# Retention and WaveMLP on one core: the first third of the instruction order written anew

## The chip, the cores and the metric

The kernel runs on one core of a Trainium2 chip. Its time is the device time of one execution in microseconds (us), as the median of several runs. The core has five engines with instruction streams of their own: PE (TensorE, the matrix unit), DVE (VectorE), ACT (ScalarE), POOL (GpSimd) and SP (SyncE, which only starts transfers here). Transfers run on 16 DMA engines and are started by SP and ACT (hardware queues) or POOL (a software queue, which here also turns float32 into bfloat16 on the way). Engines wait for each other through semaphores.

## The reference

Two layers follow each other. The first is a recurrent retention over q, k and v of shape (4 batches, 8 heads, 768 positions, 64 numbers); the second is a WaveMLP over its output, 4 x 768 x 512.

```python
for t in range(S):                                   # retention, per head, gamma = 1 - 2^(-5-h)
    state = gamma * state + outer(k[t], v[t])
    y[t] = scale * q[t] @ state
theta = x @ w_theta                                  # x: the heads side by side, 512 wide
u = x + w_tok_r @ (x * cos(theta)) + w_tok_i @ (x * sin(theta))
out = u + relu(u @ w_ch)
```

## The kernel before, in words

**Units of the retention.** The work of the retention is cut into 24 units, numbered from 0. Unit n belongs to batch n // 6, to a stretch of 256 positions ((n // 2) % 3) and to four of the eight heads (n % 2). A unit loads three tiles of 256 KB: keys (`Lk`), queries (`Lq`) and values (`Lv`), all through `load_unit` (L154 to L161). Keys and queries share a pool of 16 buffers (`kqf`), values have 9 (`vf`). The tiles are turned into bfloat16 and, where it is needed, scaled by the decay: `ck`, `cq`, `cqs` (tile `kqb`) and `cv` (tile `vb`). PE transposes keys and queries (`Tk`, `Tq`, L316), a copy `E` brings them to `kqT`, `A` (L346) makes the products of keys and queries, `m` (L355, DVE) masks them, `ST` (L373) makes the unit's contribution to the state, `S0` and `S1` add it up, `SB` writes the state as a bfloat16 matrix `sbd`, `I` (L411) applies it to the queries, and `Y` (L423) adds the part inside the unit. `XB` (a plain copy) or `XA` (a product with the decay table `qx`, L441) writes the result as half a block of `xT`.

**Blocks of the WaveMLP.** The two units 2p and 2p + 1 give two blocks of 128 positions, C = 2p and 2p + 1, over all 512 columns. For a block, `Tx` and `Ex` (or the transposing transfer `Dx`) turn `xT` round into `x_sb`; `Hh` (L469) multiplies by theta's weight; `CN` (L476, ACT) takes sine and cosine; `z` (L483) multiplies by x. The token weights are two matrices of 768 x 768. Their rows come in six transfers `Pw(r, g)` (L180 to L185, tile `row`) with r = 0 for the real, 1 for the imaginary matrix, and g = 0, 1, 2 for row blocks 0, 1 to 2 and 3 to 5. `Tw(r, t0)` (L491, tile `w_ps`) transposes one row block, `Ew` copies it. `M(t, s)` (L509, tile `y_ps`) is one of the six steps that make output block t of a batch; `u`, `Tu`, `Du`, `O` (L536), `f` and `SO` finish a block and store it. `Pth` (L173) loads theta's weight, `Pch` the channel weight. `Z` (L278) is a pair of matmuls on zeros that nothing reads.

**Constants.** `const9` and `const8` (both through L233, ACT) fill the decay table `qx` for positions 256 to 767 and 0 to 255. `const7` (L252, ACT) is a first sine, ahead of which ACT loads the table for sine.

**What sets the order.** There is no scheduler. The table `ORDER` (L22 to L86) is a list of such calls; a letter at the end of a name says which engine does it (a ACT, v DVE, p POOL, s SP). Each engine runs its instructions in the order in which the table names them, and waits with each until its inputs are there and its buffer is free. So a call that waits holds up whatever stands behind it on the same engine, its transfers too.

**Queues and buffers around the change.** The loads that SP and ACT start take eight semaphores in turn, so a load is started only when the one eight before it has landed. The weight transfers go through POOL's own queue, in the order of POOL's instructions. `th_ps`, `y_ps` and `o_ps` share two banks, so the bank of a theta product comes free when both `CN` of its block are done. The state of a unit must be in `sbd` before its `I`, and the two `SB` before it may stand on different engines.

Of the kernel before, what the change touches and what calls it, by code (L numbers as in the profile page):

```python
# [31 lines left out]
CN.0.0 Tq.5 Hh.1 Tk.5 SB.4.0.p SB.4.1.a Pw.0.1 Hh.2 m.4 E.5.v I.4 Y.4 ST.5 ck.6.a Tk.6 Tx.2 cq.6.a
CN.1.1 CN.1.0 XA.4.1 A.5 XA.4.0 m.5 Lq.9.s Ex.2.v S0.5.v z.0.p Tq.6 E.6.a CN.2.0 cv.6.p Hh.3
SB.5.0.v Tx.3 Tw.1.0 z.1.v SB.5.1.a Ew.1.0.v Ex.3.a CN.2.1 A.6 I.5 Y.5 ST.6 XA.5.0 z.2.v Tw.0.0
CN.3.0 Tx.4 CN.3.1 Ew.0.0.v S0.6.v XA.5.1 Ex.4.v Hh.4 CN.4.0 CN.4.1 Tw.0.1 M.0.1 Pw.1.1 z.3.v M.0.0
Tw.0.2 Pw.1.2 Ew.0.2.a SB.6.1.a Hh.5 z.4.p SB.6.0.p Lk.9.a M.0.3 ck.7.p cqs.7.p M.0.2 CN.5.1 CN.5.0
cq.8.a m.6 Ew.0.1.v Tw.1.1 Tw.1.2 Ew.1.1.v Lv.9.s M.0.4 M.1.0 Tx.5 Ew.1.2.v M.1.1 S1.6 Tk.7 M.1.4
Pch Ex.5.v z.5.v cv.7.v Tq.8 Tq.7 M.1.2 E.7.a M.0.5 I.6 Y.6 ST.7 A.7 ck.8.a u.0 S0.7.v m.7 XA.6.1
SB.7.1.a M.1.5 M.1.3 XA.6.0 Tw.1.3 M.2.5 Pw.0.2 M.2.3 u.1 S1.7 Tk.8 M.2.1 M.2.0 SB.7.0.v Ew.1.3.a
Tu.0 I.7 cv.8.p E.8.a cv.9.p Y.7 ST.8 A.8 cqs.9.v ck.9.v M.2.4 Du.1 Lk.10.s Eu.0.a XB.7.1.a XB.7.0.v  # L40
S0.8.v SB.8.0.v M.2.2 Tx.6 Tq.9 Tk.9 Lv.10.a cv.10.p ck.10.p Lq.10.s S1.8 u.2 m.8 O.0 E.9.a SB.8.1.a
Hh.6 Tw.1.4 I.8 Y.8 A.9 CN.6.0 Du.2 Lq.14.s CN.6.1 Ex.6.v f.0 ST.9 Tw.0.3 Hh.7 Ew.1.4.v Ew.0.3.a
S0.9.v Tw.0.4 M.3.0 Tw.1.5 CN.7.0 CN.7.1 M.3.2 Dx.7 M.3.1 M.3.5 M.3.3 Lv.12.s Lk.12.s Ew.1.5.v
XA.8.1 Ew.0.4.v Lq.12.s M.3.4 u.3 S1.9 Tw.0.5 Tk.10 M.4.5 cqs.10.p XA.8.0 m.9 M.4.3 Tq.10 SB.9.1.a
SB.9.0.a I.9 O.2 Lq.11.s Lk.11.s E.10.a Lk.15.s Ew.0.5.v Lk.14.s Y.9 ST.10 A.10 z.7.p Lv.11.s
XB.9.1.a XB.9.0.a f.2 M.4.0 O.1 M.4.1 cqs.14.p m.10 S0.10.v f.1 cq.11.a ck.12.v M.4.4 M.4.2 Tu.3
Eu.3.a Dx.9 SB.10.0.a cqs.12.p u.4 Hh.9 Tq.11 ck.11.v Tu.4 z.6.v Eu.4.v ck.15.v M.5.0 M.5.4 Tk.11
E.11.a SB.10.1.p cv.11.p M.5.2 M.5.3 I.10 M.5.5 M.5.1 Lq.13.a A.11 Y.10 ck.14.v ST.11 CN.9.1 CN.9.0
SO.0.a Hh.8 u.5 S0.11.v z.9.v XB.10.0.v m.11 Dk.12 Tx.8 Tq.14 O.4 Lv.13.a SB.11.0.a Lq.15.s Lk.13.s
CN.8.1 Lk.18.a XB.10.1.a CN.8.0 SB.11.1.p cv.12.p Lq.16.s I.11 Tk.14 Ex.8.v A.12 Y.11 ST.12 f.4  # L50
Lv.15.s O.3 z.8.p E.14.a XA.11.0 XA.11.1 Hh.10 S0.12.a f.3 SB.12.0.v Tx.10 Tu.5 CN.10.1 Dx.11
Ex.10.v cq.13.p Lk.16.s Lv.17.s Hh.11 SO.2.s CN.10.0 m.12 S1.12 z.10.v Tk.15 M.6.1 M.6.2 M.6.0 M.6.3
CN.11.0 CN.11.1 M.7.3 Lk.17.a ck.13.a M.7.4 M.7.0 M.6.4 Dk.13 M.7.1 z.11.v SB.12.1.a M.6.5 SO.3.s
A.14 M.7.2 Eu.5.v I.12 Lv.14.s u.6 cqs.15.v M.7.5 M.9.3 Tq.15 ck.17.a E.15.a m.14 SO.4.a Lq.17.s
Lq.18.s Lk.21.s ck.16.a M.9.0 M.9.5 M.9.1 M.9.4 Lq.19.a M.9.2 Du.6 cv.13.v u.7 M.8.0 u.9 Y.12
cv.14.p ST.13 A.13 O.5 cq.16.p XB.12.1.a XB.12.0.a M.8.1 S0.13.a S1.13 M.8.4 M.8.3 SB.13.0.a
SB.13.1.p m.13 I.13 ck.18.a Y.13 ST.14 A.15 f.5 cq.17.v Lv.18.a M.8.5 M.8.2 XA.13.0 XA.13.1 S0.14.v
SB.14.0.p Lv.16.s Hh.13 S1.14 u.8 Tx.12 M.10.1 cv.15.p cv.17.p SB.14.1.p M.10.0 M.10.4 cqs.18.v
M.10.5 CN.13.0 CN.13.1 Hh.12 CN.12.1 I.14 m.15 Y.14 CN.12.0 ST.15 S0.15.v XB.14.1.a SB.15.0.a M.10.3
cv.16.v Dk.16 Dk.17 Du.7 Dx.13 M.10.2 Dk.18 O.6 SB.15.1.p XB.14.0.v S1.15 I.15 Y.15 ST.16 SO.5.a  # L60
cv.18.p f.6 S0.16.v A.16 M.11.4 SB.16.1.p M.11.1 Lq.21.a Ex.12.a z.12.p SB.16.0.a Lk.19.s Lk.20.s
XB.15.0.a u.10 z.13.p XB.15.1.a m.16 O.7 Du.10 I.16 Y.16 ST.17 f.7 A.17 Tu.8 Hh.15 CN.15.1 CN.15.0
Dx.14 M.11.2 Tx.15 Lv.22.s SO.7.s M.11.0 M.11.5 S0.17.v SB.17.0.p M.11.3 XA.16.1 m.17 XA.16.0
# [24 lines left out]

# [545 lines left out]
```

## Time and profile before

| what | value |
|---|---|
| time, median of 3 runs | 165.86 us (165.68 to 165.93) |
| span of the profiled execution | 164.0 us, granted TensorE clock 0.999 |
| busy in the span: PE, DVE, ACT, POOL | 153.7, 113.1, 79.6, 76.9 us |
| read from HBM, written | 25.69 MB, 6.29 MB |
| channel of POOL's weight transfers (q0) | 3.41 MB, 12.1% of 16 DMA engines' span |
| hardware loads and stores (q1), transposing transfers (q10) | 23.73 MB, 7.47 MB |

The profile follows one execution. Its span runs from the first to the last instruction; the device time of that same execution isn't on the page, so the median stands beside the span, 1.9 us above it. A row of the timeline gives start, duration, engine, line of the code, operation, the tile written and the tiles read, and in brackets how long the engine had been idle and for whom. In a row of windows each engine has its busy time and, in brackets, its instructions; then come the granted TensorE clock, the share of the DMA engines (above 1 where transfers of several queues overlap) and GB/s. A row of the chain of waits is start, length and what the end of the program hung on in that stretch. Busy times of PE overlap from one matmul to the next, so the chain's lengths are the better measure of what a group of matmuls adds.

### The profile page before, as it was taken

The page shows a single profiled execution, that of the slowest core. Times are in us where ns is not written, and L with a number is a line of the kernel's source. Part 1 is how long each engine was busy: PE and PEld are TensorE (multiplying, and loading weights), DVE is VectorE, ACT ScalarE, POOL GpSimd, SP SyncE. Part 2 cuts the span into 40 slices and gives each one's busy share as a digit, 9 for nine tenths or more (in the row PEclk, how much of TensorE's full clock was granted, in tenths as well). Part 3 has the DMA queues.
Part 4 walks back from the last instruction along what each step waited for, and adds up shares of the span by engine and source line. Part 5 has one row for each costly group of instructions (what it writes and reads, how often), then busy time and mean ns, then how long its engine had stood idle before and what let it go on. Part 6 is the DMA issues. An engine that isn't in the chain of part 4 may idle for free.

```text
span 164.0 us, 4889 instructions
## 1 busy us (share of the span) xinstructions
PE 153.7 (94%) x2001; PEld 87.0 (53%) x2030; DVE 113.1 (69%) x210; ACT 79.6 (49%) x142; POOL 76.9 (47%) x109
## 2 busy tenths in 40 slices
PE   5997789999999999999999999999999999999992
PEld 1455556656666655654454565555555545455550
DVE  3298677977993896994879895789867760244462
ACT  4976889983658245762433725832341616000020
POOL 7957279186306733730307599951469104500000
PEclk9999999999999999999999999999999999999999
DMA  4999999999999999949999896999999438514455
GB/s 118 297 290 251 272 284 250 279 217 280 210 214 257 290 170 222 310 115 285 318 259 199 173 247 182 187 169 301 213 271 131 96 83 211 160 68 123 104 209 203
DMA packets 69062, 34.93 MB, mean 213 GB/s; under 512 B 26416, under 2 KB 66096, under 8 KB 69040
## 3 DMA queue, kind: packets, MB, share of 16 engines
q1 hardware_dynamic: 56032, 23.73, 67.4%
q10 hardware_dynamic: 10320, 7.47, 16.1%
q0 software_dynamic: 2688, 3.41, 12.1%
q8 instruction: 16, 0.26, 0.7%
q14 instruction: 6, 0.05, 0.1%
HBM read 25.69 MB, written 6.29 MB: 195 GB/s over the span
## 4 chain that ended last, share of the span: by engine, by line
PE 73%; DMA 12%; ACT 5%; POOL 4%; issue 2%; DVE 1%; DVEq 0%; SPq 0%; POOLq 0%; ACTq 0%
PE y_ps L509 35%; PE o_ps L536 12%; PE th_ps L469 9%; DMA row<-in_moe_w_tok_i_dram 5%; DMA kqf<-in_k_dram 4%; DMA kqf<-in_q_dram 4%; PE r_ps L423 3%; ACT qx L233 3%; PE at_ps L346 2%; PE r_ps L411 2%; PE kq_ps L316 2%; PE w_ps L491 2%; PE y_ps L561 2%; PE r_ps L373 1%; PE u_ps L521 1%
## 5 line engine op out<-in xcount | busy, mean ns | idle before, releaser
L509 PE MATMUL y_ps<-z,wti 128*128 128x512 bf16 x131 | 49.6, 379 | 1.0 <-issue 1.0
L509 PE MATMUL y_ps<-z,wtr 128*128 128x512 bf16 x131 | 49.7, 379 | 0.3
L483 POOL TENSOR_TENSOR z<-cs,x_sb 128x1024 bf16<-128x1024 bf16 x12 | 25.4, 2124 | 17.6 <-DMA x_sb<-xT 10.0
L355 DVE TENSOR_TENSOR at<-at_ps,mask 128x1024 bf16<-128x1024 f32 x24 | 29.2, 1216 | 0.6 <-PE at_ps L346 0.5
L308 POOL TENSOR_TENSOR vb<-vf,vsc 128x512 bf16<-128x512 f32 x17 | 18.0, 1063 | 21.3 <-DMA vf<-in_v_dram 21.0
L542 DVE SCALAR_TENSOR_TENSOR ot<-o_ps,u 128x512 f32<-128x512 f32 x23 | 15.8, 688 | 12.9 <-PE o_ps L536 12.8
L469 PE MATMUL th_ps<-wth,xT 128*128 128x512 bf16 x88 | 23.9, 379 | 0.5
L516 DVE TENSOR_TENSOR u<-y_ps,x_sb 128x512 bf16<-128x512 f32 x23 | 15.8, 688 | 12.0 <-PE y_ps L509 11.9
L536 PE MATMUL o_ps<-wch,uT 128*128 128x512 bf16 x88 | 23.2, 379 | 0.4 <-issue 0.2
L476 ACT ACTIVATE cs<-th_ps,zerob 128x512 bf16<-128x512 f32 x24 | 16.4, 684 | 12.7 <-PE th_ps L469 8.2
L476 ACT ACTIVATE cs<-th_ps,halfpi 128x512 bf16<-128x512 f32 x24 | 16.3, 684 | 10.5 <-issue 4.3
L139 POOL CAST sbd<-s 64x256 bf16<-64x256 f32 (+1 forms) x21 | 10.0, 476 | 22.9 <-DVE s L391 20.5
L509 PEld LDWEIGHTS <-wtr 128*128 128x128 bf16 x138 | 13.5, 98 | 12.7
L509 PEld LDWEIGHTS <-wti 128*128 128x128 bf16 x138 | 13.5, 98 | 11.9 <-DVE wti L139 0.2
L137 ACT COPY kqT<-kq_ps 128x1024 bf16<-128x1024 bf16 x12 | 12.1, 1012 | 10.9 <-PE kq_ps L316 10.9
L137 ACT CAST kqb<-kqf 128x512 bf16<-128x512 f32 x17 | 10.2, 619 | 8.0 <-DMA kqf<-in_k_dram 7.2
L469 PEld LDWEIGHTS <-xT 128*128 128x128 bf16 x96 | 8.9, 98 | 8.3
L536 PEld LDWEIGHTS <-uT 128*128 128x128 bf16 x92 | 8.4, 98 | 8.6
L316 PE MATMUL kq_ps<-ident,kqb 128*128 128x128 bf16 x120 | 11.2, 219 | 0.4 <-ACT kqb L137 0.2
L278 PE MATMUL zz<-zero 128*128 128x512 bf16 x27 | 9.5, 481 | 2.0 <-DVE zero L192 1.9
L423 PE MATMUL r_ps<-at,vb 64*64 64x128 bf16 x384 | 10.0, 221 | 1.1 <-DVE at L355 1.1
L316 PEld LDWEIGHTS <-kqb 128*128 128x128 bf16 x120 | 8.2, 98 | 4.5 <-POOL kqb L139 0.6
(77 smaller groups left out, 204.6 us busy)
## 6 DMA issues: line engine op xcount, KB each, us to landing
vf<-in_v_dram SPq DMA_DIRECT2D x20, 256.0 KB, 6.0
kqf<-in_k_dram SPq DMA_DIRECT2D x19, 256.0 KB, 5.3
kqf<-in_q_dram SPq DMA_DIRECT2D x17, 256.0 KB, 5.1
out_dram<-ot ACTq DMA_DIRECT2D x12, 256.0 KB, 3.0
out_dram<-ot SPq DMA_DIRECT2D x11, 256.0 KB, 3.1
kqf<-in_q_dram ACTq DMA_DIRECT2D x7, 256.0 KB, 5.4
kqf<-in_k_dram ACTq DMA_DIRECT2D x5, 256.0 KB, 5.0
vf<-in_v_dram ACTq DMA_DIRECT2D x4, 256.0 KB, 6.1
```

Of the source, the lines that this page charges most:

```text
L137: nc.scalar.copy(dst, src)
L308: engines[e].tensor_mul(in_blocks(vb), by_token(raw["vf", n]), _bcast_last(K["vsc"][:, i, :, h * HU:(h + 1) * HU], D))
L316: nc.tensor.transpose(st["kq_ps", n][:, 4 * w + x, :], st["kqb", n][:, w, x * P:(x + 1) * P], K["ident"])
L355: nc.vector.tensor_mul(at.rearrange("p g j a t -> p (g j) (a t)"), st["at_ps", n].rearrange("p g j a t -> p (g j) (a t)"), _bcast_mid(K["m ...
L423: nc.tensor.matmul(st["R", n + 1][c][g * D:(g + 1) * D, j * P:(j + 1) * P], st["vb", n][rows, lo:lo + D], st["at", n][rows, g, j, a, :], s ...
L469: nc.tensor.matmul(th_ps, st["xT", C][:, j, :], K["wth"][:, j, :], start=(j == 0), stop=(j == 3))
L476: nc.scalar.activation(st["cs", C][:, w, :], st["th_ps", C], AF.Sin, bias=K["zerob" if w else "halfpi"], scale=1.0)
L483: engines[e].tensor_mul(st["z", b][:, c], st["cs", C], _bcast_mid(x_of(C), 2))
L509: nc.tensor.matmul(st["y", t], K["wT"][r][:, s0, t0 * P:(t0 + 1) * P], st["z", b][:, s0, r, :], start=(done == 0 and r == 0), stop=(done = ...
L516: nc.vector.tensor_add(st["u", t], st["y", t], st["x", b][:, t0, :])
L536: nc.tensor.matmul(o_ps, st["uT", t][:, j, :], K["wch"][:, j, :], start=(j == 0), stop=(j == nD - 1))
L542: nc.vector.scalar_tensor_tensor(st["ot", t], st["o", t], 0.0, st["u", t], ALU.max, ALU.add)
```

## The change

The calls of the first third of `ORDER`, up to the run `A.12 Y.11 ST.12 f.4` (about 69 us in the trace of before), stand in another order. Both tables hold the same matmuls and the same number of calls; behind that point only three copies have another engine (unit 11's `XA` became `XB`, unit 12's second `XB` moved from ACT to DVE). Some calls in the first third change the engine or the form too: the plain cast of the queries (`cq`) and the scaled one (`cqs`), together with `XB` and `XA`, swap for units 1, 4, 8 and 11, and the `z` of blocks 0 and 4 moves from POOL to DVE while that of blocks 3 and 6 moves from DVE to POOL. The table has five lines fewer, so each line number below it is lower by five.

```diff
-Tk.1 E.1.a Y.0 ST.1 XB.0.1.a cqs.2.v Z.34 S0.1.v S1.1 cv.2.p SB.1.0.a Pth Lq.3.s Z.18 XB.0.0.v Tq.2
-CN.1.1 CN.1.0 XA.4.1 A.5 XA.4.0 m.5 Lq.9.s Ex.2.v S0.5.v z.0.p Tq.6 E.6.a CN.2.0 cv.6.p Hh.3
+Y.0 A.1 m.1 Lk.4.s Pth Lq.4.s cqs.3.p Lv.4.s ST.1 Lq.5.s Tk.2 XB.0.0.a cqs.2.p ck.3.p XB.0.1.a Tq.2 Z.18
+Tk.5 SB.4.0.a m.4 Tx.2 Hh.2 Lv.6.s Pw.1.1 Ex.2.v XB.3.1.a ck.6.p SB.4.1.a CN.0.1 I.4 z.1.v E.5.a Tx.3 Y.4
```

The order of the loads changes with it. Before, SP and ACT start them as Lv.0 Lk.0 Lq.0 Lv.1 Lq.1 Lk.1 Lq.4 Lk.4 Lq.2 Lk.2 Lv.2 Lq.3 Lk.3 Lv.3 Lv.4 and then unit by unit up to unit 8, whose values are called for just ahead of `E.4`. Now it is Lv.0 Lk.0 Lq.0 Lv.1 Lq.1 Lk.1 Lv.2 Lq.2 Lk.2 Lq.3 Lv.3 Lk.3 Lk.4 Lq.4 Lv.4 and on, and the loads of units 7 and 8 are called for behind the transfer `Pw.1.1`; unit 8's keys come last, on ACT, behind three loads of units 9 and 10.

On POOL, around theta's weight, the order before was this (`vb` is a unit's values in bfloat16, `kqb` its keys and queries; the number of a tile counts the tiles made, so it differs between the two kernels):

```order
L308 TENSOR_TENSOR vb_253<-vf_143,vsc_131 128x512
L308 TENSOR_TENSOR vb_317<-vf_255,vsc_131 128x512
L173 DMA wth_99<-in_moe_w_theta_dram 128x4x512
L139 CAST kqb_406<-kqf_384 128x512
L302 TENSOR_TENSOR kqb_406<-kqf_321,qsc_130 128x512
```

And now:

```order
L303 TENSOR_TENSOR vb_182<-vf_143,vsc_131 128x512
L303 TENSOR_TENSOR vb_193<-vf_177,vsc_131 128x512
L168 DMA wth_99<-in_moe_w_theta_dram 128x4x512
L297 TENSOR_TENSOR kqb_316<-kqf_226,qsc_130 128x512
L297 TENSOR_TENSOR kqb_252<-kqf_184,qsc_130 128x512
L134 CAST kqb_316<-kqf_274 128x512
L134 CAST kqb_434<-kqf_311 128x512
```

The scaled cast of unit 2's queries (kqb_252) has come to POOL, behind unit 3's; a cast of the state and the scaling of unit 1's queries, which stood on POOL ahead of the first row shown before, have left it.

On POOL again, from the first transfer of token rows on, the order before was this (row10 and row11 are the imaginary rows of block 0 and of blocks 1 and 2, row00 and row01 the real ones, row13 the imaginary rows of blocks 3 to 5):

```order
L182 DMA row10_106<-in_moe_w_tok_i_dram 128x768
L182 DMA row00_103<-in_moe_w_tok_r_dram 128x768
L139 CAST sbd00_95<-s2_427 64x4x64
L182 DMA row01_104<-in_moe_w_tok_r_dram 128x2x768
L483 TENSOR_TENSOR z_754<-cs_627,x_sb_498 128x1024
L308 TENSOR_TENSOR vb_764<-vf_467,vsc_131 128x512
L182 DMA row11_107<-in_moe_w_tok_i_dram 128x2x768
L182 DMA row13_108<-in_moe_w_tok_i_dram 128x3x768
```

And now:

```order
L177 DMA row10_106<-in_moe_w_tok_i_dram 128x768
L134 CAST kqb_563<-kqf_336 128x512
L177 DMA row00_103<-in_moe_w_tok_r_dram 128x768
L303 TENSOR_TENSOR vb_640<-vf_520,vsc_131 128x512
L177 DMA row01_104<-in_moe_w_tok_r_dram 128x2x768
L177 DMA row11_107<-in_moe_w_tok_i_dram 128x2x768
L134 CAST kqb_665<-kqf_607 128x512
L134 CAST sbd10_97<-s2_553 64x4x64
L177 DMA row13_108<-in_moe_w_tok_i_dram 128x3x768
```

Between row01 and row11 stood block 0's `z` and unit 6's values; now nothing stands there, and two casts of unit 5 have come ahead of row01.

On ACT, around the first sine, the order before was this (`kqT` is a unit's transposed keys and queries, `one` the tile of the first sine):

```order
L233 ACTIVATE qx_134<-pos_148,lscale_83,lgp_150 128x256 x4
L137 CAST kqb_193<-kqf_172 128x512
L157 DMA kqf_197<-in_q_dram 128x4x128
L157 DMA kqf_217<-in_k_dram 128x4x128
L137 COPY kqT_272<-kq_ps_240 128x1024
L137 CAST xT_306<-r_ps_260 128x256
L137 CAST sbd10_97<-s2_313 64x2x64 x2
L137 CAST kqb_308<-kqf_250 128x512
L252 ACT_TABLE_LOAD
L252 ACTIVATE one_356<-zerob_87,halfpi_85 128x1
L137 CAST xT_326<-r_ps_358 128x256
```

And now:

```order
L132 COPY kqT_358<-kq_ps_338 128x1024
L228 ACTIVATE qx_134<-pos_148,lscale_83,lgp_150 128x256 x4
L132 CAST sbd01_96<-s2_250 64x4x64
L132 COPY kqT_465<-kq_ps_381 128x1024
L132 COPY x_sb_500<-x_ps_454 128x512
L247 ACT_TABLE_LOAD
L247 ACTIVATE one_518<-zerob_87,halfpi_85 128x1
L152 DMA kqf_523<-in_q_dram 128x4x128
L132 CAST sbd11_98<-s2_362 64x4x64
```

The second part of the decay table has moved behind unit 2's copy `E` (kqT_358), and the table load with the first sine behind unit 3's (kqT_465) and block 0's `Ex`.

More of the change, by code (lines that the diff above doesn't have):

```diff
@@ L34 @@
[L34 to L63, printed above, removed]
@@ new lines @@
+SB.19.1.p SB.19.0.v M.13.0 z.17.v cqs.21.v XB.18.0.v S1.19 z.16.v cv.20.v M.12.3 M.12.2 M.13.5 Lv.21.s
+M.13.1 m.19 M.12.4 M.12.5 I.19 M.13.4 Y.19 ST.20 u.12 A.20 Dk.21 XA.19.1 S0.20.v XA.19.0 ck.22.a cq.22.a
+SB.20.1.p cv.22.p M.14.3 M.14.5 M.14.1 M.14.4 M.14.2 M.14.0 SB.20.0.p u.13 m.20 S1.20 Hh.19 I.20 Y.20
+SO.10.s Lq.23.s Lk.23.s cv.21.v u.14 A.21 ST.21 CN.19.0 CN.19.1 S0.21.v M.15.3 M.15.5 S1.21 m.21 XA.20.1
+Hh.18 CN.18.1 CN.18.0 Dx.18 Dk.22 ck.23.a M.15.4 M.15.2 SB.21.0.p M.15.1 M.15.0 SB.21.1.v Lv.23.s Du.12
@@ L86 @@
+Tuh.1 Euh.1 f.21 O.20 f.20 Oh.0 Oh.1 SO.21.a SO.22.s SO.20.s fh.0 SOh.0 fh.1 SOh.1 Z.31
 """.split()
```

81 lines of the change are left out of this document (50 added, 31 removed).

## The prediction

> **What bounds the kernel now.** I read the page's first lines, then busy time by stretches, then the chain of waits, then PE's timeline.
>
> ```profile
> span 164.0 us, 4889 instructions
> PE 153.7 (94%) x2001; PEld 87.0 (53%) x2030; DVE 113.1 (69%) x210; ACT 79.6 (49%) x142; POOL 76.9 (47%) x109
> ```
>
> PE is the bound over the whole. The windows (length; PE, PE's loads, DVE, ACT, POOL; granted clock, DMA share, GB/s) say where it is not full:
>
> ```profile
> 7.40:21.80 14.40, 11.77 (x280) 8.24 (x283) 10.46 (x20) 10.67 (x20) 8.81 (x13) 1.00 1.20 274
> 21.80:28.70 6.90, 6.62 (x112) 4.00 (x108) 5.66 (x11) 6.22 (x11) 5.99 (x8) 1.00 1.18 262
> 28.70:36.30 7.60, 7.36 (x110) 4.64 (x109) 6.21 (x15) 6.93 (x13) 3.18 (x4) 1.00 1.15 250
> 36.30:69.20 32.90, 32.13 (x511) 20.30 (x515) 26.47 (x52) 18.34 (x31) 15.67 (x17) 1.00 1.14 243
> 69.20:159.00 89.80, 88.48 (x987) 47.01 (x996) 60.32 (x105) 32.13 (x62) 37.19 (x38) 1.00 0.86 186
> ```
>
> PE idles 2.6 us up to 21.8 (matmuls on zeros are in its busy time too), then 0.3, 0.2 and 0.8 us. From 36 us on it is nearly full, so whatever the new order is to win must be won ahead of about 36 us. The DMA engines are saturated there (share 1.14 to 1.20). The chain of waits (start, length, what) leaves PE between 9.3 and 35.7 us:
>
> ```profile
> 9.27 6.62 DMA kqf<-in_k_dram
> ...
> 16.32 5.75 DMA kqf<-in_q_dram
> ...
> 22.15 1.14 ACT kqb L137 x2
> 23.28 1.17 ACT cs L476 x2
> 24.53 1.17 POOL z L483
> ...
> 26.61 0.98 POOL vb L308
> 27.60 8.04 DMA row<-in_moe_w_tok_i_dram
> ```
>
> Loads release casts on ACT, these the sine and cosine, these block 0's z on POOL, and behind that product and unit 6's values POOL starts the second imaginary rows at 27.60. They take 8.04 us. PE's timeline shows who waits for them, and four other marks:
>
> ```profile
> 20.16 0.38 PE L411 MATMUL r_ps<-kqT,sbd 128*128 128x128 bf16 x4 [0.44 <-ACT xT L137]
> ...
> 21.79 1.04 PE L469 MATMUL th_ps<-wth,xT 128*128 128x512 bf16 x3
> ...
> 32.41 0.38 PE L509 MATMUL y_ps<-z,wtr 128*128 128x512 bf16 x1
> ...
> 35.68 0.84 PE L491 MATMUL w_ps<-ident,row 128*128 128x128 bf16 x12 [0.18 <-DMA row<-in_moe_w_tok_i_dram]
> ...
> 42.82 0.39 PE L316 MATMUL kq_ps<-ident,kqb 128*128 128x128 bf16 x4
> ```
>
> These are I.3, the first theta product, the first token product, Tw.1.1 (which waits for the rows of 27.60) and unit 8's keys.
>
> **The measure.** The work of PE is the same in both kernels, so I compare its lag: the start of a mark less PE's own work ahead of it. If the lag at 36 us falls by x and the dense part stays dense, the end moves by x. What a group adds to PE is its length in the chain:
>
> ```profile
> 36.53 0.86 PE y_ps L509 x4
> 37.39 0.22 PE x_ps L455 x4
> ...
> 40.12 0.35 PE r_ps L423 x16
> 40.47 0.12 PE r_ps L373 x16
> 40.59 0.23 PE at_ps L346 x16
> ...
> 41.79 0.34 PE w_ps L491 x6
> ...
> 47.61 0.86 PE th_ps L469 x4
> ```
>
> So T, Tx and I cost 0.22, Y 0.35, ST 0.12, A 0.23, Tw 0.34, Hh 0.86, and M (two matmuls) 0.43. I leave out the zeros, which fill gaps. Before, 14 Tk and Tq (3.08), 7 ST (0.84), 7 A (1.61), 6 Y (2.10), six I of which two are half (1.10), 5 Tx (1.10), 5 Hh (4.30) and 3 Tw (1.02) stand ahead of the first token product: 15.15 us, a lag of 32.41 - 15.15 = 17.26. Up to Tw.1.1 come 4 M, a Tw and an Hh, 2.92: the lag is 35.68 - 18.07 = 17.61. Now one Tw fewer stands ahead of the first token product (14.81), and 3 M, 2 Tw, an Hh and a Tx (3.05) stand between, 17.86 in all.
>
> **The change, part by part.**
>
> *Loads and theta's weight.* All bytes still come, at the same rate. Unit 2 and unit 3 come in order where unit 4 had come ahead of unit 2, and theta's weight is issued about 2.5 us sooner. By the rows below it would land near 17 us instead of 12.54 + 6.8 = 19.3; its first reader, Hh.1, I put near 20.4. Before, Hh.0 at 21.79 did not wait for it either, so I cost this at nothing; what hides it is the retention of units 2 and 3. The price is that unit 3's keys land some 3 us later, about 16.4 by my count of 0.9 us a load (256 KB at 274 GB/s), near the time when E.3 wants them.
>
> ```profile
> 12.54 0.93 POOL L173 DMA_DIRECT2D wth<-in_moe_w_theta_dram  x1
> ```
> ```profile
> wth<-in_moe_w_theta_dram POOLq DMA_DIRECT2D x1, 512.0 KB, 6.8
> ```
>
> *ACT.* The second part of the decay table and the table load now lie between E.2 and I.3:
>
> ```profile
> L476 ACT ACTIVATE cs<-th_ps,zerob 128x512 bf16<-128x512 f32 x6 | 4.1, 683 | 0.0
> L137 ACT COPY kqT<-kq_ps 128x1024 bf16<-128x1024 bf16 x4 | 4.0, 1011 | 1.4 <-PE kq_ps L316 1.4
> ...
> L233 ACT ACTIVATE qx<-pos,lscale,lgp 128x256 f32<-128x256 f32 x4 | 2.1, 584 | 0.0
> ...
> L137 ACT COPY x_sb<-x_ps 128x512 bf16<-128x512 bf16 x3 | 1.8, 585 | 0.0
> L137 ACT CAST sbd<-s 64x256 bf16<-64x256 f32 x4 | 1.6, 402 | 2.1 <-DVE s L391 2.1
> ...
> L137 ACT CAST xT<-r_ps 128x256 bf16<-128x256 f32 x4 | 1.5, 370 | 0.1
> ```
> ```profile
> 13.05 1.28 ACT L252 ACT_TABLE_LOAD   x1
> 14.35 0.29 ACT L252 ACTIVATE one<-zerob,halfpi 128x1 f32<-128x1 f32 x1
> ...
> 33.81 0.80 ACT L137 COPY wtr<-w_ps 128x768 bf16<-128x768 bf16 x1 [0.36 <-PE w_ps L491]
> ```
>
> I put unit 2's transposed queries at 13.6, so E.2 ends near 15.0 and the decay table near 17.0. SB.2.0 and the keys of unit 3 let E.3 start near 17.7. From there ACT has E.3 1.01, Ex.0 0.59, the table load 1.28 and the first sine 0.29, SB.3.0 0.40, two XB 0.74 and SB.3.1 0.40: 4.71 us, ending at 22.4, or 22.2 since neighbours overlap a little. I.3 then starts at 22.2 against 20.16, 2 us later. But Hh.1 now stands ahead of it, and PE's work from I.3 to the first token product is smaller: I 0.66, Y 1.05, ST 0.36, A 0.69, four Hh 3.44, four T 0.88, three Tx 0.66, two Tw 0.68 = 8.42, which alone gives 30.6. ACT decides instead: a token product needs a bank that CN.3.0 frees, and behind SB.3.1 ACT has eight CN (5.46), three XB (1.11), three SB (1.20), two E (2.02) and a weight copy (0.80): 10.6 us. One after the other that ends at 32.8; with starts about 0.1 us sooner than the ends before them, at 31.0. ACT was busy 6.93 of 7.60 us in 28.7 to 36.3, so waits are few; I take 31.7, with 31.0 and 32.8 as ends. The lag there is 31.7 - 14.81 = 16.89 against 17.26, a gain of 0.37.
>
> *Rows.* Without z.0 and unit 6's values ahead of it, Pw.1.1 is issued at about 25.0 instead of 27.60. Its price is 8.04, so it would land near 33.0, up to 36.1 if it shares the engines with more loads (an estimate: 3 us more). Tw.1.1 wants it at 31.7 + 3.05 = 34.75. Were it there, the lag would be 16.89 and the gain 17.61 - 16.89 = 0.72. The two preceding real rows are wanted 0.86 us behind the first token product and may be late too, so I leave 0.22 us for these waits: gain 0.50.
>
> *z and casts between POOL and DVE.* z.0 left the chain, where it cost 1.17 us. Its reader, the first token product, comes at 31.7, and DVE (5.66 of 6.90 us busy in 21.8 to 28.7) has it done by then: nothing. A z on DVE behind late sines could hold a mask and with it a Y; that belongs to the ends above.
>
> *Units 7 and 8.* Behind unit 8's keys stand ck.8 and Tk.8. Up to these keys 30 loads (7.86 MB), theta's weight (0.52) and five row transfers (1.77) must come: 10.16 MB. At 274 GB/s and less in the windows above (3.95, 1.81 and 1.90 MB from 7.4 to 36.3) and about 1.5 MB ahead of 7.4 (an estimate, three quarters of the rate behind it), 9.1 MB are there at 36.3, and the rest at 243 GB/s at 40.6. With a cast on POOL of 0.6 us (an estimate between the copies above) Tk.8 could start at 41.3. Before it started at 42.82, with the gain it is wanted near 42.4. So I cost it at nothing, with about 1 us to spare.
>
> **Sum.** -0.37 at the first token product, -0.35 that the rows no longer add, +0.22 for row waits: -0.50. The executions' span is 164.0 and the median 165.86, 1.9 around it, which both kernels have: 163.5 and 165.4.
>
> **A rule against it.** The five row transfers and the loads meet on the same DMA engines. From 31.4 to 36 us (packets, MB, share of the engines), and one load issued there (KB, us to landing):
>
> ```profile
> q0 software_dynamic: 501, 0.75, 88.9%
> q1 hardware_dynamic: 542, 0.27, 26.3%
> ...
> kqf<-in_k_dram ACTq DMA_DIRECT2D x1, 256.0 KB, 6.9
> ```
>
> While rows are under way, the loads get 0.27 MB in 4.6 us, a fifth of the 1.3 MB that they would get alone at 274 GB/s. The Trainium skill ("DMA: Bandwidth & Descriptors", "Queues, rings and completion order") says that each DMA engine takes turns between its queues packet by packet. The trace agrees: 501 and 542 packets, though the row packets carry three times the bytes. By that rule the loads of units 7 and 8, now called for behind the rows, cannot push ahead, and unit 8's keys come late; that is the first rival.
>
> **The rivals.**
> - *R1, slower: unit 8's keys are late.* If Pw.1.2 and the next rows (Pw.0.2) run back to back from 33 to about 40 us (1.18 MB at 0.75 MB in 4.6 us is 7.2 us), the loads get 0.42 MB in that time. Unit 8's keys and the three loads ahead of them are 1.05 MB, so 0.6 MB are left, 2.3 us at 274 GB/s: landing near 42.5 and Tk.8 at 43.3, in the worst case 44.5. For it speaks that the load issued in that stretch took 6.9 us; against it that eight loads are under way by then. It decides from a landing at about 41.8 on. A wait of 0.7 to 2 us, less the gain: 166.1 to 167.4, at its middle 166.7. Chance 0.20.
> - *R2, slower: ACT bounds the stretch up to 32 us.* If E.3 waits for unit 3's keys to 19 us, I.3 starts at 23.5 and the first token product at 33 instead of 31.7; beyond 32.1 nothing is gained there. With 0.6 to 1.3 us more than I took: 166.0 to 166.7, at its middle 166.3. For it speaks that the decay table, the table load and the first sine (3.7 us) stand between E.2 and I.3 on ACT; against it that Hh.1 fills PE. Chance 0.16.
> - *R3, no change: the rows come as late as before.* If the second imaginary rows land at 35.5 all the same, because the ones ahead take the queue, the lag is as before: 165.9. For it speaks the 0.75 MB in 4.6 us. Chance 0.12.
> - *R4, more gain:* no wait for rows and ACT at its lower end, 31.0: 17.61 - (31.0 - 14.81) = 1.4 us at most, 164.4. Chance 0.06.
>
> **How the numbers follow.** A measurement tells about 0.2% (0.33 us) from no change. My forecast, 165.4, has 0.40 for itself, about 165.0 to 165.7; with R4 faster holds 0.44 after taking off 0.02 for its edge at 165.53. R3 and these edges are the 0.14 of no change. R1, R2 and 0.06 for a stall that I don't see (the stretch from 43 to 69 us is written anew too, where PE idles 0.8 us; or a granted clock below the 1.00 of all windows) make slower 0.42. The range goes from R4's end, 164.4, to R1's, 167.4; the likeliest alone has 165.0 to 165.7.
>
> **What would show it.** In the profile of the changed kernel: the table load between 19 and 21 us; I.3 near 22.2 and the first token product near 31.7, ahead of 32.41; the second imaginary rows issued near 25.0 and no idle time ahead of Tw.1.1, at about 35.0; Tk.8 near 42.4 with no idle time, and PE's idle time from 36 to 69 us at 0.8 us or less. I am wrong if I.3 comes behind 23, if a wait for kqf or kqb of unit 7 or 8 stands on PE between 37 and 44 us, or if the windows behind 43 us show new idle time on PE.

## The result and the profile after

The changed kernel takes 167.08 us (166.90 to 167.13, 4 runs) beside 165.77 us for the kernel before in the same runs: a ratio of 1.0081 (95% interval 1.0067 to 1.0096), 1.3 us slower. The prediction said 165.4 and faster. The profiled execution has a span of 165.4 us against 164.0; it is the one of the four with a low granted clock (0.99 on average; the others have 0.997 to 1.00, and take 166.90 to 167.13 us like it).

The first lines of the page after, with the granted clock in 40 slices:

```profile
span 165.4 us, 4921 instructions
PE 156.2 (94%) x2030; PEld 87.1 (53%) x2030; DVE 114.1 (69%) x206; ACT 81.0 (49%) x145; POOL 79.1 (48%) x110
...
PEclk9996999999999999999999999999999999999999
```

Busy shares are as before; PE has 2.5 us more, partly because the trace of before holds 29 matmul records fewer. New is the 6 in the fourth slice of the clock. The windows after, in the columns of the prediction:

```profile
7.40:21.80 14.40, 12.00 (x247) 7.58 (x247) 9.68 (x18) 9.72 (x17) 9.42 (x12) 0.88 1.21 278
21.80:28.70 6.90, 5.71 (x140) 3.81 (x138) 5.94 (x13) 6.63 (x15) 5.39 (x10) 1.00 1.19 280
28.70:36.30 7.60, 7.30 (x109) 4.66 (x107) 6.05 (x13) 6.35 (x10) 3.54 (x4) 1.00 1.16 224
36.30:43.00 6.70, 6.68 (x92) 3.99 (x91) 4.76 (x9) 2.55 (x4) 2.01 (x4) 1.00 1.16 273
43.00:69.20 26.20, 26.10 (x375) 15.91 (x373) 21.86 (x40) 17.14 (x30) 14.69 (x13) 1.00 0.96 217
```

PE idles 1.2 us from 21.8 to 28.7 us where it had idled 0.3, and ahead of 21.8 its matmuls run at a clock of 0.88 on average. From 36 us on it is full. So the loss too lies ahead of 36 us. PE's timeline has the waits; these are the ones over 0.5 us, and then the first token product and Tw.1.1 (the last row):

```profile
9.55 0.42 PE L341 MATMUL at_ps<-kqT 64*64 64x128 bf16 x16 [0.67 <-ACT kqT L132]
11.63 0.62 PE L311 MATMUL kq_ps<-ident,kqb 128*128 128x128 bf16 x8 [1.12 <-ACT kqb L132]
...
23.14 0.40 PE L406 MATMUL r_ps<-kqT,sbd 128*128 128x128 bf16 x4 [0.63 <-ACT sbd L132]
28.44 0.51 PE L486 MATMUL w_ps<-ident,row 128*128 128x128 bf16 x6 [0.56 <-DMA row<-in_moe_w_tok_i_dram]
...
33.44 0.38 PE L504 MATMUL y_ps<-z,wtr 128*128 128x512 bf16 x1
...
36.49 0.50 PE L486 MATMUL w_ps<-ident,row 128*128 128x128 bf16 x6
```

With the prediction's own counts the lag at the first token product is 33.44 - 14.81 = 18.63 against 17.26, 1.37 us more, and the span is 1.4 longer. At Tw.1.1 it is 36.49 - 17.86 = 18.63 against 17.61: no wait for the second imaginary rows any more, but 1.0 us more lag; the other 0.4 us come behind it, with no single wait that stands out. The chain of waits names what came before each (its longer pieces):

```profile
4.79 5.62 DMA kqf<-in_k_dram
...
10.44 1.15 ACT kqb L132 x2
...
18.54 0.41 POOL sbd L134
...
19.02 1.04 POOL vb L303
20.07 0.97 POOL kqb L297
21.03 0.98 POOL vb L303
22.01 6.39 DMA row<-in_moe_w_tok_i_dram
...
28.44 0.52 PE w_ps L486 x6
...
31.55 1.85 ACT cs L471 x3
...
33.44 1.02 PE y_ps L504 x4
```

Two transfers stand in it that the sum didn't have. The first is unit 1's keys. Before, SP started them at 2.40 us and they landed at 8.76; now ACT starts them behind the first part of the decay table, at 4.79, behind the values of unit 2 and the queries of unit 3 on the DMA engines, and they land at 10.41. PE waits 1.12 us for their cast (the line of 11.63 above). The second is the first imaginary rows (row10). POOL waits 2.89 us with unit 2's state cast for the state, and three products stand between that cast and the transfer, which lands at 28.40 instead of 26.45.

```profile
18.54 0.40 POOL L134 CAST sbd<-s 64x256 bf16<-64x256 f32 x1 [2.89 <-DVE s L386]
```

Two corrections to the text ahead of the prediction. In the table of the profile before, the queue q10 is ACT's queue (28 loads and stores there before, 32 after, with 7.47 and 8.52 MB), not the transposing transfers. And the order of the loads that the text on the change gives is that of the calls in the table, not that of the starts. In the trace of before, ACT starts unit 4's queries and keys only at 8.79 and 9.27, behind the decay table and behind the starts of unit 2's and unit 3's queries and keys (5.18 to 8.30). In the trace after, unit 1's keys stand ahead of unit 2's values and unit 3's queries in the table, but those are started at 2.41 and 4.56 and the keys at 4.79.

### The profile page after: what moved, and what is told of

Read it like the earlier page. It is cut to its first block, busy times and chain, and to the rows that moved or that the text cites. A ratio compares the mean times of both kernels' runs of the same rounds, so it can differ in the third digit from the quotient of the medians.

```text
span 165.4 us, 4921 instructions
## 1 busy us (share of the span) xinstructions
PE 156.2 (94%) x2030; PEld 87.1 (53%) x2030; DVE 114.1 (69%) x206; ACT 81.0 (49%) x145; POOL 79.1 (48%) x110
## 3 DMA queue, kind: packets, MB, share of 16 engines
q10 hardware_dynamic: 12816, 8.52, 18.1%
q0 software_dynamic: 2688, 3.41, 11.7%
## 4 chain that ended last, share of the span: by engine, by line
PE 78%; DMA 7%; ACT 4%; POOL 4%; DVE 3%; issue 1%; DVEq 0%; ACTq 0%; POOLq 0%
PE y_ps L504 36%; PE o_ps L531 12%; PE th_ps L464 9%; DMA row<-in_moe_w_tok_i_dram 4%; PE r_ps L418 4%; PE kq_ps L311 3%; DMA kqf<-in_k_dram 3%; PE at_ps L341 3%; PE w_ps L486 2%; PE r_ps L406 2%; PE y_ps L556 2%; PE r_ps L368 2%; POOL vb L303 1%; ACT cs L471 1%; ACT kqT L132 1%; PE x_ps L450 1%
## 5 line engine op out<-in xcount | busy, mean ns | idle before, releaser
L504 PE MATMUL y_ps<-z,wtr 128*128 128x512 bf16 x138 | 52.4, 380 | 0.2
L504 PE MATMUL y_ps<-z,wti 128*128 128x512 bf16 x138 | 52.4, 379 | 0.0
L464 PE MATMUL th_ps<-wth,xT 128*128 128x512 bf16 x96 | 24.5, 379 | 0.0
L471 ACT ACTIVATE cs<-th_ps,zerob 128x512 bf16<-128x512 f32 x24 | 16.4, 686 | 12.8 <-PE th_ps L464 7.8
L132 ACT CAST kqb<-kqf 128x512 bf16<-128x512 f32 x15 | 9.1, 618 | 9.3 <-DMA kqf<-in_k_dram 9.3
L132 ACT COPY kqT<-kq_ps 128x1024 bf16<-128x1024 bf16 x11 | 11.1, 1010 | 3.4 <-PE kq_ps L311 3.4
L273 PE MATMUL zz<-zero 128*128 128x512 bf16 x30 | 10.9, 501 | 1.9 <-DVE zero L187 1.9
L132 ACT CAST xT<-r_ps 128x256 bf16<-128x256 f32 x21 | 7.4, 371 | 9.3 <-DVE s L386 6.5
```

The costliest lines, as they stand in the source:

```text
L132: nc.scalar.copy(dst, src)
L273: nc.tensor.matmul(t, K["zero"][:, :P], K["zero"], start=True, stop=True)
L464: nc.tensor.matmul(th_ps, st["xT", C][:, j, :], K["wth"][:, j, :], start=(j == 0), stop=(j == 3))
L471: nc.scalar.activation(st["cs", C][:, w, :], st["th_ps", C], AF.Sin, bias=K["zerob" if w else "halfpi"], scale=1.0)
L504: nc.tensor.matmul(st["y", t], K["wT"][r][:, s0, t0 * P:(t0 + 1) * P], st["z", b][:, s0, r, :], start=(done == 0 and r == 0), stop=(done = ...
```

## The experiments

In each of these a few calls of the table are moved. The edits are shown as words of the table ("..." for what stands between); where an edit is in two places, both are shown: a call that is moved is missing in one place and stands in the other. The times are medians beside the kernel before in the same runs, whose median was 165.6 to 165.8.

### Each suspected piece alone

```diff
-const9 cv.0.p Lk.1.a
+const9 Lk.1.s cv.0.p
```

> The changed kernel with one load moved: unit 1's keys are started by SP ahead of unit 0's values cast (as the kernel before had it), not by ACT behind the first part of the decay table. Three theories for the 1.3 us. K (keys): unit 1's keys land at 10.4 instead of 8.8 us, so PE loses 2.4 us at unit 1's transposes and never gets half of it back; then this run gains 0.6 to 1.0 us on the changed kernel, about 166.2. C (ACT): the decay table and the table load between E.2 and I.3 set the time of I.3; then it gains 0.3 at most, 166.8. W (rows): POOL starts the first imaginary rows only at 22.0 and PE waits for them at 28.4; then it gains nothing, 167.0.

Measured: 166.33 us (166.09 to 168.23, 9 executions), ratio 1.0068 (1.0034 to 1.0101). Seven executions took 166.1 to 166.7 with a clock of 1.00, two 168.1 and 168.2 with 0.986. K holds: keys that land at 8.68 instead of 10.41 win 0.8 us. But two executions with a low clock lose some 2 us more. The traced execution is one of those; in windows of its slow stretch, from about 15.2 to 18.6 us, the clock (last but two) is

```profile
14.00:16.00 2.00, 1.33 (x23) 0.67 (x21) 1.08 (x5) 1.83 (x4) 1.24 (x2) 0.80 1.25 251
16.00:18.00 2.00, 2.00 (x36) 1.16 (x38) 1.18 (x1) 1.17 (x3) 0.00 (x0) 0.50 1.18 216
18.00:20.00 2.00, 2.00 (x36) 1.39 (x28) 1.15 (x4) 1.35 (x3) 1.17 (x2) 0.84 1.16 324
```

The loss goes through the rows: POOL starts them at 22.22 and they land at 29.49, where the same kernel with the clock held (below, with one pair of zeros) has 21.09 and 27.11; the first token product comes at 34.54 against 32.16.

ACT's two pieces:

```diff
-ck.4.p const8 ... ST.3 const7
+Lq.2.a Lk.2.a const8 ... cq.1.a const7 A.0
```

> The changed kernel with ACT's two pieces put early: the second part of the decay table right behind the loads that ACT starts (as in the kernel before, ahead of E.0), and the table load with the first sine behind unit 1's casts. Unit 1's keys still land at 10.4. C: 2.1 + 1.6 us less on ACT between E.2 and I.3, so I.3 comes 1 us or more sooner and 0.6 to 1.0 us of the loss goes, about 166.2. K: 167.0, since PE waits for the keys as before and E.0 is not on that path. W: 167.0 too, the rows come as late.

Measured: 167.06 us, ratio 1.0091 (1.0074 to 1.0107): nothing won. The trace says why. I.3 came 1.0 us sooner, at 22.17, and PE then waited for the same rows at the same time:

```profile
22.17 0.39 PE L409 MATMUL r_ps<-kqT,sbd 128*128 128x128 bf16 x4
...
28.43 0.51 PE L489 MATMUL w_ps<-ident,row 128*128 128x128 bf16 x6 [0.71 <-DMA row<-in_moe_w_tok_i_dram]
```

The rows:

```diff
-S1.2 cv.3.p ... cv.4.p S0.3.v Pw.1.0
+S1.2 Pw.1.0 cv.3.p ... cv.4.p S0.3.v
```

> The changed kernel with the first imaginary row transfer started three POOL products sooner (ahead of the values of unit 3, near 19 instead of 22.0). W: Tw.1.0 doesn't wait at 28.4 any more and 0.5 to 0.7 us are won, about 166.4. K and C: the wait only hides lag that was there already, 166.9 to 167.1; more rows beside the loads could even cost 0.2.

Measured: 166.80 us, ratio 1.0077 (1.0060 to 1.0095), about 0.3 us below the changed kernel. The transfer started at 18.90, the first row transposes came at 27.88 without a wait, and the next transposes waited 0.44 us for the real rows. I.3 was as late as in the changed kernel (23.02), so W has a part, not the whole.

```profile
27.88 0.51 PE L488 MATMUL w_ps<-ident,row 128*128 128x128 bf16 x6
...
30.14 0.51 PE L488 MATMUL w_ps<-ident,row 128*128 128x128 bf16 x6 [0.44 <-DMA row<-in_moe_w_tok_r_dram]
```

The clock:

```diff
-A.0 Z.11
+A.0 Z.11 Z.40 Z.41 Z.42
```

> The changed kernel with three more pairs of matmuls on zeros behind the pair that follows A.0, in PE's idle time from 10 to 11.6 us; nothing else is moved. In the trace of the changed kernel the granted clock falls to 0.50 from about 14 to 17 us. Theory H (clock): that idle time drops the clock and the slow stretch costs; then this run keeps 1.00 and gains 0.5 us or more, 166.5 or less. Rival: PE has idle time to spare there and waits for ACT and POOL at 23 us all the same; then the clock stays at 1.00 and the time is 167.0 to 167.2.

Measured: 167.13 us, ratio 1.0088 (1.0064 to 1.0112), clock 1.00 in all four. The clock alone isn't the loss; the three executions of the changed kernel at 0.997 to 1.00 say the same. With the zeros I.3 came at 22.36, 0.8 us sooner, and the wait for the rows grew from 0.56 to 1.37 us:

```profile
22.36 0.40 PE L409 MATMUL r_ps<-kqT,sbd 128*128 128x128 bf16 x4 [0.63 <-ACT sbd L135]
...
28.47 0.51 PE L489 MATMUL w_ps<-ident,row 128*128 128x128 bf16 x6 [1.37 <-DMA row<-in_moe_w_tok_i_dram]
```

### Pieces together

Keys and one pair of zeros (the edit of the keys above, and `Z.11 Z.40`):

> The run with unit 1's keys started by SP, with one more pair of zeros behind the pair that follows A.0. That run took 166.1 to 166.7 with the clock at 1.00 and 168.1 to 168.2 with 0.986. H: the pair keeps the clock up and all executions lie near 166.2. Rival: the idle time that drops it lies elsewhere (12.2 to 13.5 and 14.4 to 15.2 us too), so some executions stay at 168.

Measured: 166.44 us (165.94 to 166.53, 7 executions), ratio 1.0040 (1.0026 to 1.0055), clock 1.00, no execution near 168. The keys are worth 0.7 us.

Rows and three pairs of zeros, keys left late:

> The changed kernel with three pairs of zeros (clock at 1.00) and the first imaginary rows three POOL products sooner; unit 1's keys stay late. With zeros alone, PE was 0.8 us ahead at I.3 and lost it again waiting for the rows at 28.4. Theory S (series): late keys and low clock matter because the state cast of unit 2 on POOL waits for them and the rows stand behind it; with the rows in front of that, the 0.8 us last, and the time is 166.1 to 166.4. Rival: the next wait takes them (ACT's copies and z behind the rows); then 166.7 or more, as with the rows alone.

Measured: 166.44 us (166.25 to 166.50), ratio 1.0045 (1.0028 to 1.0061). The rows are worth 0.7 us once the clock is up, against 0.3 without. In the trace PE now waits 0.72 us for the next rows, the real ones of block 0, whose start was not moved.

Keys, rows and one pair of zeros:

> Unit 1's keys by SP, the rows three POOL products sooner, one pair of zeros; ACT's pieces stay late. If ACT's pieces cost nothing once keys, clock and rows are right, this is as fast as the run with all parts, 165.7 to 165.9. If they do cost (I.3 at 22.0 against 20.2 in the kernel before), it stays at 166.2 to 166.4 as without the sooner rows.

Measured: 165.78 us, nine of ten executions at 165.6 to 165.9 and one at 167.8 with a clock of 0.986; ratio 1.0022 (0.9997 to 1.0047). So the two together give back nearly all that the change lost: 167.1 with zeros alone, 0.7 for the one, 0.7 for the other. Against the kernel before in the same runs 0.2 us is left, which this interval doesn't tell from nothing; the two runs below that have the keys and the rows early as well (1.0018 and 1.0012) have intervals that lie above 1, so a rest of 0.2 to 0.3 us is likely. In the trace I.3 and the first token product come at

```profile
21.98 0.40 PE L409 MATMUL r_ps<-kqT,sbd 128*128 128x128 bf16 x4
...
31.93 0.38 PE L507 MATMUL y_ps<-z,wtr 128*128 128x512 bf16 x1
```

which is a lag of 17.12, 0.14 below the kernel before.

With ACT's pieces early as well:

> Unit 1's keys by SP, ACT's pieces early, first rows sooner, and one more pair of zeros. If the three together are what the change lost, this reaches the kernel before: 165.6 to 165.9. If a part lies elsewhere (units 7 and 8 at 38 to 40 us cost 0.3 by the lag), it stays 0.3 to 0.5 above, near 166.1.

Measured: 165.88 us, ratio 1.0018 (1.0005 to 1.0030), no better. Late pieces on ACT cost nothing in this order once the keys and the rows come early. And ACT's pieces with the rows, keys late and no zeros:

> Both edits that gave little alone: ACT's two pieces early, and the first imaginary rows three POOL products sooner. In the run with ACT's pieces early, I.3 came 1 us sooner but PE waited for the rows at 28.4 as before; in the run with the rows sooner that wait was gone, but I.3 was late. Theory S (series): the two stand behind each other and each hides the other's gain; then together they gain 0.8 to 1.1 us on the changed kernel, 166.0 to 166.3. Rival: loads or z behind them are late anyway; then no more than the 0.3 of the rows alone, 166.8.

Measured: 166.64 us (165.80 to 167.10, 10 executions), ratio 1.0054 (1.0034 to 1.0073). Six executions had a clock of 0.99 and took 166.6 to 167.1, four had 1.00 and took 165.8 to 166.5: where the rows no longer hide it, the low clock costs 0.7 us. The four at 1.00 (median 166.0) lie 0.4 us below the four with rows and zeros and ACT's pieces late (166.44). With the keys late, then, these pieces may have a price of their own; the two sets overlap, and it isn't settled.

Two pairs of zeros with keys and rows:

> Unit 1's keys by SP and the first rows three POOL products sooner, with two pairs of zeros instead of one. With one pair nine executions took 165.6 to 165.9 and one, with the clock at 0.986, 167.8. Theory: two pairs keep the clock at 1.00 in all of them and cost nothing, since PE waits there for unit 1's casts: 165.6 to 165.8, no slow one, within 0.2% of the kernel before. Rival: the second pair delays unit 1's transposes by 0.3 us: 166.0.

Measured: 165.97 us (165.75 to 166.28, 11 executions), ratio 1.0012 (1.0003 to 1.0021), clock 0.996 to 1.00. No execution near 168 any more, and no price of the second pair that shows: the median is 0.1% above the kernel before, as with one pair.

| kernel | I.3 | Tw.1.0 | first token product | its lag | ratio |
|---|---|---|---|---|---|
| changed | 23.14 | 28.44 | 33.44 | 18.63 | 1.0081 |
| zeros | 22.36 | 28.47 | 33.47 | 18.66 | 1.0088 |
| ACT early | 22.17 | 28.43 | 33.44 | 18.63 | 1.0091 |
| rows | 23.02 | 27.88 | 32.88 | 18.07 | 1.0077 |
| rows, zeros | 22.37 | 27.07 | 32.68 | 17.87 | 1.0045 |
| keys, zeros | 22.05 | 27.16 | 32.16 | 17.35 | 1.0040 |
| keys, rows, zeros | 21.98 | 26.82 | 31.93 | 17.12 | 1.0022 |
| all three, zeros | 22.04 | 26.87 | 32.26 | 17.45 | 1.0018 |
| before | 20.16 | 28.78 | 32.41 | 17.26 | 1 |

I.3 moves by a microsecond without moving the end as long as the first rows are late: the table's second and third rows. (Tw.1.0 stands behind more work in the order before.)

### The same pieces put into the kernel before

Unit 1's keys started by ACT:

```diff
-const9 Lk.1.s cv.0.p
+const9 Lk.1.a cv.0.p
```

> The kernel before with one load moved: unit 1's keys are started by ACT behind the first part of the decay table, as in the changed kernel, not by SP. K: PE's first gap grows by 1.5 to 2 us at unit 1's transposes and the clock falls, so it loses 0.5 to 1.2 us: 166.1 to 166.8. Rival: the kernel before has 0.5 to 0.8 us of waits at each unit there that take it up: 165.6 to 165.8.

Measured: 165.69 us (165.50 to 166.70, 10 executions), ratio 1.0017 (1.0000 to 1.0033). The forecast loss didn't come, and the reason is not the rival's. Issued at 4.79 as in the changed kernel, the keys landed at 8.60, as early as before, since no other new load stood ahead of them. What makes them late in the changed kernel is the two loads that are started ahead of them there (2.41 and 4.56, landing at 8.61 and 9.52), not the engine.

ACT's pieces late:

```diff
-Z.39 const8 ck.0.p ... Tk.2 const7 I.1
+SB.2.1.a const8 Z.11 ... Ex.0.a const7 cv.3.v
```

> The kernel before with ACT's two pieces late, as in the changed kernel: the second part of the decay table behind unit 2's second state cast, the table load with the first sine behind block 0's Ex. C: 3.7 us more on ACT between A.2 and I.3, so I.3 comes 1 to 2 us later than 20.2, and 0.5 to 1.0 us are lost: 166.1 to 166.6. Rival: ACT waits 1.7 and 2 us there anyway, and PE waits for the sixth unit's casts at 22.8 whatever comes first: 165.6 to 165.8.

Measured: 171.59 us (169.86 to 171.69), ratio 1.0333 (1.0283 to 1.0383). In the order before, the same pieces that cost nothing in the new one (keys and rows early) cost 6 us, the fall of the clock that came with them included (0.98 in all four executions). The trace (of the execution of 169.9 us) has E.3 behind the decay table, 2 us of waiting on PE, a low clock from 20 us on, and I.3 at 23.08 instead of 20.16; the other three executions took 1.7 us more, and none of them left a trace:

```profile
20.17 0.58 PE L314 MATMUL kq_ps<-ident,kqb 128*128 128x128 bf16 x4 [2.01 <-ACT kqT L135]
...
23.08 0.59 PE L409 MATMUL r_ps<-kqT,sbd 128*128 128x128 bf16 x4 [0.58 <-ACT xT L135]
```
```profile
PEclk9999858999999999999999999999999999999999
```

### The gain that the prediction saw

The second imaginary rows sooner, in the kernel before, first by 3.5 us:

```diff
-S0.5.v z.0.p ... M.0.1 Pw.1.1 z.3.v
+S0.5.v Pw.1.1 z.0.p ... M.0.1 z.3.v
```

> The kernel before with one call moved: the second imaginary rows are started ahead of block 0's z and unit 6's values on POOL, at about 24 instead of 27.6. This is the gain that the prediction put on the change, alone. If the rows were the bound at 35.7, it gains 0.3 to 0.4 us on the kernel before, 165.4. If PE makes up for that wait behind it, or the z and the values come later by the time of the issue, it is the same within 0.1 us, 165.8.

Measured: 166.74 us (165.96 to 167.50, 8 executions), ratio 1.0069 (1.0042 to 1.0096): slower, and scattered. A second set with a trace of another execution:

> The kernel before with the second imaginary rows 3.5 us sooner, as in the earlier run, to see an execution of another length. In the one with a trace (165.96) unit 7's keys landed at 37.2 instead of 32.2, just in time. L: in an execution near 167 they land at 38.5 or later and PE waits 0.5 to 1.3 us for them ahead of unit 7's transposes. P: they land as before and the lost time lies between 22 and 30 us, on z and its readers.

Measured: 166.20 us (165.56 to 167.49, 8 executions), ratio 1.0040 (1.0014 to 1.0066). Both traces are of short executions. In both, POOL waits for unit 7's keys, which land at 37.2 and 36.8 us instead of 32.2; this is the cast in the second:

```profile
36.88 0.61 POOL L137 CAST kqb<-kqf 128x512 bf16<-128x512 f32 x1 [1.09 <-DMA kqf<-in_k_dram]
```

So the rows take the DMA engines from the loads that are started beside them, as in R1, one unit sooner. There the keys come just in time. That a later landing makes the long executions is argued from this, not shown, since none of them left a trace.

By 1 us only:

```diff
-CN.2.0 cv.6.p ... M.0.1 Pw.1.1 z.3.v
+CN.2.0 Pw.1.1 cv.6.p ... M.0.1 z.3.v
```

> The kernel before with the second imaginary rows started between block 0's z and unit 6's values, about 1 us sooner than before; the run that started them 3.5 us sooner was 0.7% slower and scattered from 166.0 to 167.5. Theory L (loads starve): the sooner the rows, the longer unit 7's keys take, since they are started within the same microseconds; at 1 us sooner the loads of unit 7 are under way by then, so it is between 165.4 and 166.0. Rival P (POOL): the loss came from z and values that stood behind the issue; here the z is ahead of it and only values come later by 0.7 us, so it is 165.4 to 165.6, faster than before by the part of the row wait that goes.

Measured: eight of ten executions at 165.17 to 165.51 beside 165.8, one at 166.9 and one at 168.8; ratio 0.9982 (0.9963 to 1.0002). The trace is of the one at 168.8, where unit 5's values were scaled in 2.6 us on DVE instead of 0.7; it says nothing on the others. Once more:

> The kernel before with the second imaginary rows between block 0's z and unit 6's values, once more, with more executions and a trace: eight of ten executions took 165.2 to 165.5 beside 165.8 for the kernel before, two took 166.9 and 168.8. If the wait at 35.68 is gone and nothing takes its place: 165.4, 0.2% faster, no idle time on PE ahead of Tw.1.1 and unit 7's keys not later than 36. If the scatter is L's, unit 7's cast waits for its keys as in the runs with the rows 3.5 us sooner.

Measured: 165.72 us, ratio 1.0025 (0.9997 to 1.0053): eight of twelve executions at 165.15 to 165.90, four at 166.7 to 167.4. The traced one (span 163.6) shows the forecast gain, Tw.1.1 without a wait at 35.22 instead of 35.68:

```profile
35.00 0.38 PE L507 MATMUL y_ps<-z,wti 128*128 128x512 bf16 x1
35.22 0.83 PE L489 MATMUL w_ps<-ident,row 128*128 128x128 bf16 x12
```

So the wait that the prediction wanted to win does go, but what that is worth isn't settled: the eight short executions had a median 0.5 us below the kernel before in the first set (165.31 beside 165.80) and 0.1 below in the second (165.52 beside 165.58), and the rest lost over 1 us. This is no better kernel. With block 0's z on DVE as well:

> The same, and block 0's z on DVE, as the changed kernel has it, so that POOL starts the second imaginary rows at about 24.5. L: about as soon as in the run that moved the rows ahead of the z, so the same scatter, 165.5 to 167.5, median 166.2 or more. P: z was the only trouble with the rows ahead of it; with the z on DVE it is as fast as with the rows 1 us sooner, 165.2 to 165.5.

Measured: 166.55 us (166.43 to 166.66), ratio 1.0051 (1.0034 to 1.0068), without scatter. Neither theory had that: PE waits 0.92 us for a state cast of unit 5 at 30.59, which is a new wait on ACT. It doesn't tell L from P.

## Why the prediction was wrong, point by point

- **Loads, costed at nothing: the step that failed first.** It took the order of the table for the order of the starts. It priced unit 3's keys, at 3 us later (16.4); they landed at 14.03 against 13.30. It passed over unit 1's, which the table doesn't move back but the trace does. They land 1.65 us later, PE waits 1.12 us, and with the clock held the runs put 0.7 us on it. What was to hide the loads, the retention of units 2 and 3, lies behind these keys. Theta's weight, issued 2.8 us sooner, landed no sooner (19.77 against 19.38, not near 17), 1.1 us ahead of Hh.1 at 20.83: costed at nothing rightly, but with a third of the room.
- **Rows: right on the one that it looked at, blind to the one ahead.** Pw.1.1 was issued at 25.48 (forecast 25.0) and landed at 35.06 (33.0 to 36.1, and near R3's 35.5), and Tw.1.1 doesn't wait. That is in part luck: the forecast wanted these rows at 34.75, and they held nothing up because Tw.1.1 came at 36.49. With keys and rows put right they landed at 34.06, ahead of Tw.1.1 at 34.98. But the lag there was no longer theirs to give: Pw.1.0 stands behind unit 2's state cast and three products on POOL, landed at 28.40 and held Tw.1.0. That is the other 0.7 us. I named what left the queue ahead of Pw.1.1, and not what stands ahead of Pw.1.0.
- **ACT: about right for I.3, wrong on what I.3 decides.** I.3 was put at 22.2; it came at 23.14, at 22.36 with the clock held (0.63 us of waiting for a cast on ACT), and at 21.98 to 22.05 with the keys early too, so the working on ACT was right to 0.2 us and its inputs were late. The last agreement is luck as well: with ACT's pieces out of the way too (c_all) I.3 comes at 22.04 all the same. And ACT didn't decide the first token product, as the sum had it: the rows did. First token product: forecast 31.7 (31.0 to 32.8), measured 33.44, and 31.93 with keys and rows put right. R2 named nearly the measured times (23.5 and 33), with ACT as the cause; taking ACT's pieces away alone moved I.3 by 1.0 us and the end by nothing.
- **The clock** stood in the last 0.06. In the traced execution it fell to 0.50 for 3.4 us, by windows of half a microsecond from about 13.8 to 17.2; no wait of PE ahead of it is longer than 1.12 us. In the changed kernel the late rows hide it; with the rows right it costs 0.7 us where it falls at about 11.6 (c_act_row), and with the keys early 2 us where it falls at 15.2 (a_key_sp). That the place makes the difference is argued, not shown. The Trainium skill ("TensorE: Matmul & The Clock Gate", Part 1, "What's actually happening") has the clock fall after an idle window of about 3.4 us. The length of the slow stretch agrees; the cause doesn't, as PE was never idle that long: it was busy 1.93 of the 3.41 us ahead of the fall (0.88 of 2.00 us from 10 to 12).
- **R1** did not happen: unit 8's keys landed at 41.93 (forecast 40.6), past the 41.8 from which R1 was to decide, but Tk.8 came at 44.94, not 42.4, so nothing waited for them. Its mechanism is real, though: the runs with sooner rows in the kernel before show it at unit 7.
- **z and casts**, costed at nothing: z.0 was done in time. f_half_z shows that the same move in the order before makes a new wait.
- **Sum.** -0.37 at the first token product became +1.37; the -0.35 behind it was real in the trace (no wait at Tw.1.1) and far smaller than what came ahead. The +0.22 for the real rows fell away in the changed kernel, whose imaginary rows were later still; in the runs with the first rows sooner the real ones cost 0.18 to 0.73 us of waiting, or nothing (c_all).

## What to carry to other kernels

When transfers are reordered, follow the first transfers that PE needs, not those that waited before: a queue's first item and what waits ahead of its issue instruction on the issuing engine decided here. Waits in series hide each other: of four suspects taken away one at a time, only one (the keys, 0.8) won more than 0.3 us, and two together, with the clock held, won 1.1 of the 1.3. A piece's price belongs to its place in the order: 3.7 us on ACT cost nothing in one order with its loads and rows put right, and 6 us, a fall of the clock included, in the other.

## What the runs showed of the hardware

- In the traces with a fall of the clock under way (the changed kernel, a_key_sp, a_act_early, a_row_early, c_act_row, b_act) it stayed at half for 3.4 us, in b_act for 6.8, from a start between 11.6 and 15.2 us (b_act 19.7). In the 3.41 us ahead PE was busy 1.93 us in the changed kernel and 1.44 to 1.59 in the others, in waits of 1.24 us and less (b_act 2.0). That alone doesn't decide: in the traced execution of e_row_half PE was busy 0.77 of the 3.41 us from 24.90, with one wait of 2.64, and the clock stayed at 1.00. What decides was not settled. Without zeros and with late keys 14 of 22 executions had a clock of 0.99 or less; with three pairs of zeros in one wait none of 8 (c_zero, d_row_zero). With the keys early it was 2 of 9 without zeros (a_key_sp), one of 27 with one pair and none of 11 with two.
- A row transfer started 0.7 us sooner landed no sooner: 22.01 to 28.40 in the changed kernel, 21.29 to 28.43 with zeros. With zeros and the keys early, 21.09 to 27.11. Started at 18.90 it landed at 24.43. What holds it was not settled.
- A load that ACT started 2.4 us later landed at the same time (4.79 to 8.60 against 2.40 to 8.76), so here the order among the loads counted and the moment of issue didn't.
